# A fused attention and rational feed-forward kernel: first values in eight pieces by pairs of heads, products ordered by pairs, two small vectors from GpSimd's queue

## The chip, the cores and the metric

The kernel runs on one core of one Trainium2 chip. The metric is the device time of one execution in microseconds, as the median over several runs. Matrix products run on TensorE (PE in the profile, PEld for its weight loads), elementwise work on VectorE (DVE) and ScalarE (ACT), small set-up work on GpSimd (POOL). SyncE (SP) only issues loads and stores; ScalarE and GpSimd can issue them too, each from a queue of its own.

## The reference

The inputs are q, k and v of shape (4 batches, 4 heads, 1088 positions, 32), two sketch matrices S1 and S2 of shape (8, 32), two weight matrices w_in (128, 2048) and w_out (2048, 128), and two short vectors a (4 numbers) and b (2 numbers).

```python
def phi(x):
    a = np.einsum('rd,bhsd->bhsr', S1, x)
    b = np.einsum('rd,bhsd->bhsr', S2, x)
    return np.einsum('bhsi,bhsj->bhsij', a, b).reshape(*x.shape[:-1], r * r)
q_p, k_p = (phi(q), phi(k))
kv = np.einsum('bhsf,bhsd->bhfd', k_p, v)
z = np.sum(k_p, axis=2)
num = np.einsum('bhsf,bhfd->bhsd', q_p, kv)
den = np.einsum('bhsf,bhf->bhs', q_p, z)[..., None] + 1e-06
x = num / den            # then heads side by side: (4352, 128)
h = x @ w_in
P = a[0] + a[1] * h + a[2] * h**2 + a[3] * h**3
Q = 1.0 + np.abs(b[0]) * np.abs(h) + np.abs(b[1]) * h**2
out = (P / (Q + 1e-06)) @ w_out
```

The attention has no softmax: each batch first sums its keys and values into one small matrix (kv, with z as one more column), and then each query is multiplied by it.

## The kernel before

The kernel is written as named steps, and a long list, `ORDER` (L21 to L57), says in which order they are issued. A step `name:i` of the list calls one method for unit or block i. Every engine executes its own instructions strictly in the order of that list, and waits on semaphores for what another engine or a load has still to deliver. Nothing is reordered when the kernel runs.

**Keys** (class `Keys`). Batch 0 is treated in three parts of 2, 2 and 5 tile groups. `kt` transposes pieces of k on VectorE (L254); `ks` multiplies them by the sketch matrices on TensorE (L261); `kc` copies one half of the sketches on ScalarE (L268); `kf` multiplies both halves into the features k_p on VectorE (L273); `kp` multiplies features and values on TensorE and sums into kv (`products`, `add`, L302). `kk` copies kv to SBUF on ScalarE (tile kvz, L312). For batch 0 kv has two banks, one for each pair of heads (c = 0 and 1), and `kp0`, `kp1`, `kp2` each do one part for both pairs.

**Queries** (classes `Queries` and `Spread`). Blocks 0, 1, 2 of batch 0 have 256 positions each, block 3 has 320. `qt` transposes on VectorE (L325), `qs` sketches on TensorE (L338, for later blocks L409), `qc` copies on ScalarE (L345, L348, L415), `qf` makes the features on VectorE, `qp` multiplies by kvz (L365), `qd`, `qi`, `qx` divide (L373, L380, L385), `qb` transposes back on TensorE (L391), `qk` copies the result into xT on ScalarE (L398).

**Feed-forward.** Tokens come in units of at most 512. `h0` to `h3` compute quarters of the hidden layer on TensorE (L455, two wide PSUM buffers), `e0` to `e3` copy them to bf16 on ScalarE (L461); `u`, `w`, `y` form Q on VectorE; `ln`, `ex` form 1/Q on ScalarE; `pa`, `pd`, `s`, `m`, `v`, `x` form the terms of P/Q; `G` multiplies by w_out on TensorE (L588), `st` stores. The steps `wo:0` to `wo:5` (`w_part`) make the scaled bf16 copies of w_out, on ScalarE or VectorE by a table; `wo:0`, `wo:2`, `wo:4` use the first half of w_out, the others the second half. The step `ba` takes the absolute value of b (tile b_abs) on ScalarE.

**The opening.** Before the list, the loads of S1, S2, k, the first 512 columns of q, a, b and v are issued (L138 to L159). k comes in three loads over ScalarE's and SyncE's queues; then SyncE issues q and the four pieces of v (one for each quarter of the partitions, all four heads, `load_v`), and ScalarE issues a and b. GpSimd meanwhile fills masks and constants, and, when the sketch matrices are there, makes S21 (L206) and SAB (L212), the weights of the query sketches. The list then issues, on SyncE, the two halves of w_out (`lw:1`, `lw:0`), the rest of q (`lq:0`), the halves of w_in (`lx:1`, `lx:0`) and the loads of later batches (`lk`, `lv`, `lq`). The step `tn` (L167 to L170) runs matmuls on an empty tile, whose number is in `TURNS`, so that TensorE is not idle while the first loads are under way.

Completion of loads is counted on eight semaphores that the framework hands out in turn, over both hardware queues together. So a load is issued only when the load eight places before it has landed; on the queue of its engine, everything behind it waits too. Loads issued from GpSimd have counters of their own.

## Time and profile before

| what | value |
|---|---|
| median of 3 runs | 272.62 us (272.51 to 272.63) |
| profiled execution, whole | 272.61 us |
| its span, first to last instruction | 270.8 us |
| mean granted TensorE clock | 0.994 |
| busy time TensorE / VectorE / ScalarE / GpSimd | 257.7 / 256.7 / 248.8 / 2.9 us |
| busy in the first 10 us: TensorE / VectorE / ScalarE | 8.40 / 5.29 / 2.27 us |
| busy from 10 to 20 us: TensorE / VectorE / ScalarE | 9.95 / 7.65 / 5.02 us |
| moved by loads, 0 to 10 us and 10 to 20 us | 174 and 326 GB/s |

Busy time is a sum over all instructions of an engine. TensorE's includes the idle matmuls of the opening, and its matmuls overlap, so that a busy TensorE need not run at its peak. The profile's rows give start and length of an instruction (or of several of one line, merged), the line of the kernel, the operation, the tiles that it writes and reads, and in brackets how long the engine stood idle before it and what ended that. The chain of waits is read backwards: from the last instruction to what released it, and so on to the start; it is printed in order of time.

### The profile page before, as it was taken

What the parts mean: (1) busy time and instruction counts of PE and PEld (TensorE: products, weight loads), DVE (VectorE), ACT (ScalarE), POOL (GpSimd) and SP (SyncE); (2) the same over time, 40 slices, a digit from 0 to 9 for tenths busy, and PEclk for the clock granted to TensorE, in tenths of its full rate; (3) what the DMA queues carried; (4) which work ended last, traced back from release to release, by engine and by line L of the source; (5) the groups of instructions that cost most, each with busy time, mean ns of one, the idle gap of its engine ahead of it and who ended that gap; (6) DMA issues with size and microseconds to landing.
All of it is one profiled execution on the core that took longest, in us unless ns stands there. A gap on an engine that the chain in (4) does not pass through costs nothing.

```text
span 270.8 us, 3732 instructions
## 1 busy us (share of the span) xinstructions
PE 257.7 (95%) x1382; PEld 147.5 (54%) x1397; DVE 256.7 (95%) x278; ACT 248.8 (92%) x224; POOL 2.9 (1%) x24
## 2 busy tenths in 40 slices
PE   8999999999999899999999999999999999999683
PEld 3787556864645344635464554444545356675372
DVE  3777999999999999999999999999999999999994
ACT  1268999998999999999999999999999999999991
POOL 4000000000000000000000000000000000000000
PEclk9999999999999999999999999999999999999889
DMA  6995614333230044231304000400034200020005
GB/s 167 265 323 151 156 38 136 117 90 96 76 106 34 12 118 100 77 75 33 97 6 123 7 0 3 119 11 0 15 97 73 43 0 0 2 39 1 0 2 79
DMA packets 30530, 19.55 MB, mean 72 GB/s; under 512 B 20400, under 2 KB 26672, under 8 KB 30512
## 3 DMA queue, kind: packets, MB, share of 16 engines
q1 hardware_dynamic: 28864, 18.92, 26.9%
q10 hardware_dynamic: 1648, 0.40, 0.8%
q8 instruction: 11, 0.18, 0.3%
q14 instruction: 7, 0.06, 0.1%
HBM read 16.16 MB, written 3.15 MB: 71 GB/s over the span
## 4 chain that ended last, share of the span: by engine, by line
ACT 47%; PE 34%; issue 8%; DVE 5%; DMA 4%; SPq 0%; ACTq 0%; DVEq 0%
PE h_ps L455 16%; ACT ln L546 13%; ACT r L550 12%; ACT hh L461 12%; PE att_ps L588 10%; ACT p L541 7%; PE att_ps L365 3%; DMA v_sb<-in_v_dram 2%; PE att_ps L302 2%; DMA k_sb<-in_k_dram 2%; DVE g L558 2%; DVE s L554 1%; ACT xT L398 1%; PE att_ps L391 1%; PE att_ps L409 1%
## 5 line engine op out<-in xcount | busy, mean ns | idle before, releaser
L455 PE MATMUL h_ps<-xT,w_in_sb 128*128 128x512 f32 (+1 forms) x320 | 125.8, 537 | 2.8 <-ACT hh L461 1.9
L455 PEld LDWEIGHTS h_ps<-xT,w_in_sb 128*128 128x128 f32 x320 | 58.3, 190 | 55.2 <-issue 37.3
L461 ACT CAST hh<-h_ps 128x1024 bf16<-128x1024 f32 x68 | 67.5, 1027 | 3.5 <-PE h_ps L455 3.1
L588 PEld LDWEIGHTS <-w_out 128*128 128x128 bf16 x460 | 45.5, 100 | 45.9 <-issue 14.3
L546 ACT ACTIVATE ln<-w 128x2048 f32<-128x2048 bf16 (+1 forms) x35 | 66.0, 1887 | 0.7 <-DVE w L495 0.6
L550 ACT ACTIVATE r<-ln 128x2048 bf16<-128x2048 f32 (+1 forms) x35 | 65.8, 1880 | 0.6 <-PE att_ps L588 0.2
L541 ACT ACTIVATE p<-hh,a_sb 128x2048 bf16<-128x2048 bf16 (+1 forms) x23 | 46.7, 2035 | 0.1
L554 DVE TENSOR_TENSOR s<-hh,r 128x2048 bf16<-128x2048 bf16 (+2 forms) x33 | 41.0, 1246 | 0.2 <-ACT r L550 0.2
L495 DVE TENSOR_TENSOR w<-w,u 128x4096 bf16<-128x4096 bf16 (+2 forms) x22 | 39.4, 1798 | 0.1
L588 PE MATMUL att_ps<-g,w_out 128*128 128x512 bf16 (+1 forms) x154 | 34.8, 350 | 4.3 <-DVE g L569 3.9
L558 DVE TENSOR_TENSOR g<-hh,s 128x2048 bf16<-128x2048 bf16 (+1 forms) x30 | 35.2, 1175 | 0.0
L569 DVE TENSOR_TENSOR g<-g,p 128x2048 bf16<-128x2048 bf16 (+1 forms) x30 | 35.1, 1178 | 0.1
L588 PE MATMUL att_ps<-r,w_out 128*128 128x512 bf16 (+1 forms) x154 | 34.8, 353 | 0.3
L588 PE MATMUL att_ps<-s,w_out 128*128 128x512 bf16 (+1 forms) x137 | 29.3, 342 | 0.2
L490 DVE TENSOR_SCALAR w<-u,b_abs 128x4096 bf16<-128x4096 bf16 (+2 forms) x22 | 23.8, 1090 | 0.0
L484 DVE TENSOR_SCALAR u<-hh 128x4096 uint16<-128x4096 uint16 (+2 forms) x22 | 21.4, 976 | 1.6 <-ACT hh L461 1.5
L365 PEld LDWEIGHTS att_ps<-kvz,q_pT 128*128 128x128 f32 x144 | 17.7, 191 | 4.6 <-issue 2.0
L365 PE MATMUL att_ps<-kvz,q_pT 128*128 128x66 f32 x144 | 17.9, 273 | 0.1
L302 PEld LDWEIGHTS att_ps<-v_sb,k_p 128*64 128x64 f32 (+1 forms) x288 | 8.8, 138 | 1.9 <-DVE qT L325 0.8
L536 DVE TENSOR_SCALAR p<-hh,a_sb 128x2048 bf16<-128x2048 bf16 x12 | 9.7, 808 | 0.0
L302 PE MATMUL att_ps<-v_sb,k_p 128*64 128x64 f32 (+1 forms) x288 | 9.2, 223 | 0.5 <-DMA v_sb<-in_v_dram 0.5
L273 DVE TENSOR_TENSOR k_p<-att_ps,b_sk 128x1024 f32<-128x1024 f32 (+2 forms) x8 | 9.3, 1178 | 0.1
(60 smaller groups left out, 134.3 us busy)
## 6 DMA issues: line engine op xcount, KB each, us to landing
a_all<-sk_d SPq DMA_DIRECT2D x6, 384.0 KB
b_all<-sk_d SPq DMA_DIRECT2D x12, 192.0 KB
v_sb<-in_v_dram SPq DMA_DIRECT2D x12, 144.0 KB
k_sb<-in_k_dram SPq DMA_DIRECT2D x3, 544.0 KB
q_sb<-in_q_dram SPq DMA_DIRECT2D x3, 544.0 KB
a_all<-sk_d SPq DMA_DIRECT2D x4, 320.0 KB
b_all<-sk_d SPq DMA_DIRECT2D x8, 160.0 KB
w_out_sb_f<-in_moe_w_out_dram SPq DMA_DIRECT2D x2, 512.0 KB
```

What stands on the lines that cost most here:

```text
L365: nc.tensor.matmul(self.nd[:, o:o + 2 * KW], lhsT=self.q_p[:, c, x:x + 128], rhs=kvz[self.b % 2][:, c, :], start=True, stop=True)
L455: nc.tensor.matmul(t[:, x * tl:(x + 1) * tl], lhsT=w_in_sb[:, f * 128:(f + 1) * 128], rhs=xT[:, x_at(t0):x_at(t0) + tl], start=True, stop= ...
L461: nc.scalar.copy(out=live[i]["hh"][:, part * PW:(part + 1) * PW], in_=live[i]["h", part])
L490: nc.vector.tensor_scalar(out=t[:, c], in0=live[i]["u"][:, c], scalar1=ab1, scalar2=ab0, op0=AX.mult, op1=AX.add)
L495: nc.vector.tensor_mul(out=t[:, c], in0=t[:, c], in1=live[i]["u"][:, c])
L541: nc.scalar.activation(out=part_of(i, "p", h), in_=hh, func=ACT.Identity, scale=a3, bias=a2)
L546: nc.scalar.activation(out=t, in_=live[i]["w"][:, span(h)], func=ACT.Ln, bias=1.0 + 1e-6)
L550: nc.scalar.activation(out=part_of(i, "r", h), in_=live[i]["ln"], func=ACT.Exp, scale=-1.0)
L554: nc.vector.tensor_mul(out=part_of(i, "s", h), in0=hh, in1=part_of(i, "r", h))
L558: nc.vector.tensor_mul(out=part_of(i, "g", h), in0=hh, in1=part_of(i, "p" if horner(i, first(h)) else "s", h))
L569: nc.vector.tensor_mul(out=g, in0=g, in1=part_of(i, "s" if horner(i, first(h)) else "p", h))
L588: nc.tensor.matmul(outs[t0][:, :tl], lhsT=w_sb[y][:, f0 + x, :], rhs=part_of(i, key, h)[:, c:c + tl], start=done[0] == 0, stop=done[0] == ...
```

## The change

The first batch's values come in eight loads instead of four: each quarter of the partitions is split by pairs of heads. The four pieces of the first pair are issued before q, two from SyncE and two from ScalarE; the four pieces of the second pair are issued after q, all from SyncE. a and b are issued from GpSimd, behind the making of the identity matrix and ahead of S21 and SAB. `products` for batch 0 now does the first two parts for the first pair of heads (`kp0`), all three parts for the second pair (`kp2`), and the third part for the first pair (`kp1`); in the list `kp2` stands ahead of `kp1`.

In the list, `tn` has 9 + 2 = 11 idle matmuls instead of 11 + 2 = 13. `ks:0` stands ahead of `ks:1`, all key sketches and the features of the first two parts ahead of the first query's transpose and sketch, which now stands between `kp0` and `kp2`. The first half of w_out is loaded behind both halves of w_in; `wo:0`, `wo:2` and `wo:4`, which use it, stand later. `ba` stands ahead of the copy `qc:0`. Between there and the middle of the second unit some neighbours change places (the hidden quarters h1 and h0, the query blocks 5 and 6, `ln0:0` ahead of `kc1:1`); after that, single neighbours on different engines are exchanged, and three times two neighbours on ScalarE. The constant `VH` is not used.

```diff
-TURNS = (11, 0, 0, 0, 2, 0, 0, 0, 0)
+TURNS = (9, 0, 2, 0, 0, 0, 0, 0, 0)
 ORDER = """
-tn:4 tn:0 lw:1 lq:0 kt0:0 lw:0 kt1:0 lx:1 kt2:0 lx:0 ks1:0 kt3:0 ks0:0 lk:1 qt:0 ks2:0 kc0:0 kc1:0 kf0:0 kf1:0 qs:0
-kc2:0 qt:1 kf2:0 qc:0 kp0:0 ba:0 kp1:0 qf:0 kp2:0 wo:3 qs:1 kk:0 lv:1 qt:2 qp:0 qc:1 wo:1 qf:1 qs:2 qd:0 qi:0 qc:2
-qp:1 qx:0 qf:2 wo:0 qb:0 qp:2 qd:1 qi:1 qk:0 qx:1 qt:3 h3:0 qd:2 qi:2 lq:1 qx:2 wo:4 wo:2 h2:0 e3:0 kt1:1 h0:0 kt0:1
-e2:0 pa1:0 u1:0 lk:2 qs:3 w1:0 qb:2 h1:0 y1:0 qc:3 qk:2 e0:0 qt:5 qb:1 ks0:1 qt:4 e1:0 qs:4 qk:1 u0:0 ln1:0 h1:1 qt:6
...
+tn:0 lw:1 lq:0 tn:2 kt1:0 lx:1 kt0:0 lx:0 kt2:0 ks0:0 lw:0 ks1:0 kt3:0 kc0:0 lk:1 ks2:0 kf0:0 kc1:0 kf1:0 kp0:0 kc2:0
+qt:0 kf2:0 qs:0 ba:0 kp2:0 qt:1 qc:0 qf:0 kp1:0 wo:3 qs:1 kk:0 lv:1 qt:2 qp:0 qc:1 wo:1 qf:1 qs:2 qd:0 qi:0 qc:2 qp:1
+qx:0 qf:2 qb:0 qt:3 qp:2 qk:0 qd:1 lq:1 qi:1 h2:0 qd:2 qi:2 wo:2 wo:0 h3:0 wo:4 e2:0 qx:2 qx:1 kt1:1 qs:3 e3:0 kt0:1
+h1:0 pa1:0 u1:0 lk:2 w1:0 h0:0 y1:0 e1:0 qb:2 qt:4 qc:3 qb:1 e0:0 ks0:1 qt:6 qk:1 qs:4 u0:0 qk:2 ln1:0 h1:1 qt:5 w0:0
...
+    v0 = v[0].rearrange("h (g j) d -> g h (j d)", g=32)
+
+    def first_v(c):
+        for m in range(NM):
+            w = min(W, (NJ - m * NT) * D)
+            hs = slice(2 * c, 2 * c + 2)
+            (nc.scalar if c == 0 and m % 2 else nc.sync).dma_start(out=v_bufs[0][m * 32:(m + 1) * 32, hs, 0:w],
+                                                             in_=v0[:, hs, m * W:m * W + w])
+
     q0 = io.tile([128, S], FP, name="q_sb", bufs=1)
     q0_src = q[0].rearrange("h (g j) d -> (h g) (j d)", g=32)
+    first_v(0)
     nc.sync.dma_start(out=q0[:, 0:512], in_=q0_src[:, 0:512])
+    first_v(1)
     a_sb = consts.tile([128, 4], FP, name="a_sb")
     b_sb = consts.tile([128, 2], FP, name="b_sb")
-    nc.scalar.dma_start(out=a_sb, in_=bass.AP(tensor=moe_a.tensor, offset=moe_a.offset,
-                                              ap=[[0, 128]] + list(moe_a.ap)))
-    nc.scalar.dma_start(out=b_sb, in_=bass.AP(tensor=moe_b.tensor, offset=moe_b.offset,
-                                              ap=[[0, 128]] + list(moe_b.ap)))
     nc.scalar.preload_act_table_set("natural_log_exp_and_others")
-    load_v(0)
...
     make_identity(nc, ident)
+    nc.gpsimd.dma_start(out=a_sb, in_=bass.AP(tensor=moe_a.tensor, offset=moe_a.offset,
+                                              ap=[[0, 128]] + list(moe_a.ap)))
+    nc.gpsimd.dma_start(out=b_sb, in_=bass.AP(tensor=moe_b.tensor, offset=moe_b.offset,
+                                              ap=[[0, 128]] + list(moe_b.ap)))
...
             if self.first:
-                t0, n = self.PARTS[part]
-                self.add(part, range(t0, t0 + n), (0, 1))
+                for x in ((0, 1), (2,), (0, 1, 2))[part]:
+                    t0, n = self.PARTS[x]
+                    self.add(x, range(t0, t0 + n), (part // 2,))
```

## The prediction

> **What bounds the kernel now.** The profiled execution took 272.61 us, 270.8 us of it span and 1.8 us around it; the median of the three runs is 272.62 us, so a sum made against the profiled execution stands for the median too. I first read the page's table of slices and the busy time by stage:
>
> ```profile
> ACT  1268999998999999999999999999999999999991
> DMA  6995614333230044231304000400034200020005
> ```
>
> From the fourth slice on (slices are 6.8 us), ScalarE is nearly never free; between 30 and 50 us it is busy for 20.00 of 20 us, VectorE for 19.94. ScalarE's waits between 17 and 60 us are those for hidden layers at 19.60 and 21.33 and 0.2 us for a denominator. Saturated engines run the same work whenever they start, so what the opening gains or loses by about 21 us goes to the end one for one, unless something there comes at a fixed time. So next I read the chain of waits over the first 18 us (start, length, what):
>
> ```profile
> 1.48 4.35 DMA k_sb<-in_k_dram
> 5.83 0.02 issue
> 5.85 3.92 DMA v_sb<-in_v_dram
> 9.77 0.28 issue
> 10.05 2.32 PE att_ps L302 x72
> 12.37 1.06 PE h_ps L338 x8
> ...
> 17.66 0.40 PE h_ps L455
> ```
>
> k lands at 5.83, the last piece of v is issued in that moment and lands at 9.77; TensorE takes up the key products (L302) 0.28 us later and has no gap from there to the first hidden layer (L455). The timeline shows the work between:
>
> ```profile
> 5.00 0.15 PEld L170 LDWEIGHTS <-idle 128*128 128x128 bf16 x1 [0.28 <-issue]
> 5.07 1.62 DVE L254 STREAM_TRANSPOSE kT<-k_sb 128x256 f32<-128x256 f32 x4 [1.46 <-DMA k_sb<-in_k_dram]
> 5.43 0.15 PEld L170 LDWEIGHTS <-idle 128*128 128x128 bf16 x1 [0.27 <-issue]
> 6.41 1.00 PE L261 MATMUL att_ps<-S,kT 128*128 128x64 f32 x8
> 7.12 0.45 DVE L325 STREAM_TRANSPOSE qT<-q_sb 128x256 f32<-128x256 f32 x1 [0.43 <-DMA q_sb<-in_q_dram]
> 7.24 1.28 PE L261 MATMUL h_ps<-S,kT 128*128 128x64 f32 x10
> 7.69 1.29 DVE L273 TENSOR_TENSOR k_p<-att_ps,b_sk 128x512 f32<-128x512 f32 x2
> 8.45 1.13 PE L338 MATMUL h_ps<-qT,SAB 64*128 64x256 f32 x8
> 9.25 1.45 DVE L273 TENSOR_TENSOR k_p<-h_ps,b_sk 128x1280 f32<-128x1280 f32 x1
> 10.05 2.32 PE L302 MATMUL att_ps<-v_sb,k_p 128*64 128x64 f32 x72 [0.46 <-DMA v_sb<-in_v_dram]
> ```
>
> Two things can go: the 0.46 us for which TensorE waits for v, and its late start at 6.41, behind idle matmuls (L170), although the first two transposes (0.77 of the 1.62 us) are over at 5.84.
>
> **The change, step by step.** *Two idle matmuls fewer.* Their weight loads stand 0.43 us apart (5.00, 5.43), so idling ends up to 0.86 us sooner; the transposes let the sketches start at about 5.90: 0.51 us gained. The sketches take 6.41 to 8.45, 2.04 us, and end at 7.95.
>
> *Features before the query.* VectorE ends its transposes at 6.69. The first sketches now fill the first part alone, so its copy (L268, about 0.2 us) is done near 6.85, and both features are made by 6.9 + 1.29 = 8.2. Only then comes the query's transpose, to 8.2 + 0.37 (0.45 less its overlap) = 8.57. The wait for q of 0.43 us disappears if q lands by 8.2; it landed at 7.1 and has half of the first four v pieces, 144 KB, put ahead of it, 0.5 us at the 291 GB/s moved from 5.5 to 6.0 us. The large feature then ends at 8.57 + 1.45 = 10.02 instead of 10.70.
>
> *Products by pairs.* Half of the pieces now stand ahead of q, two on each queue, no longer behind k's landing. Their bytes lie right behind k's, so I put their landing near 7; TensorE wants them at 8.0. The eight products of two tile groups are done by about 8.5 (second feature 8.2). The query sketch starts at 8.63, takes its slot of 1.06 (chain, 12.37) and ends at 9.69. There remain 56 of 72 records; the stage fills 10.05 to 12.29, where the next begins, so 31 ns each: 1.74 us, to 11.43. The large feature sets no later end: 40 records after 10.02 is 11.3. Before, the end was 12.29: 0.86 us gained at most.
>
> *The last piece of v.* Each load is issued when the load eight places before it has landed, as the fourth piece was, at 5.85. The last two now follow the first v piece and the rest of k. I put that piece at 6.2 to 6.4 (k's 5.83 and half a piece: the second load of v moved its four in the 2.4 us from 52.8 to 55.2, 0.3 us each half), so the last issue starts at about 6.8. From an issue's start to use I have two rows: about 2.0 us in the second load (last issue at 53.2, data moving until 55.2) and 3.92 in the chain. That gives 8.8 to 10.7; I take 9.55, nearer the lower, as pieces are half as large and less stands ahead. With the chain's 0.28 us, products restart at 9.83, end at 11.57: a gain of 0.72 us. The ends of the range are 0.86 (landing by 9.4) and 12.29 - (10.98 + 1.74) = -0.43.
>
> A rule against it stands in the Trainium skill, "DMA: Bandwidth & Descriptors", section Bandwidth: under 64 KB a transfer costs mostly its fixed part, 64 KB taking 0.95 us and 1 MB 6.15. By it, as an estimate, eight pieces of 72 KB take 8.0 us and four of 144 KB 5.6, 2.4 more if nothing overlaps. In the second load four such pieces moved in 2.4 us all told, so pieces overlap and the trace does not agree.
>
> *a and b from GpSimd.* Their two issue slots on ScalarE's queue (0.45 and 0.44) go to two pieces of v: nothing saved there. On GpSimd they stand before S21 and SAB (L206, L212). No row shows a load issued there; by the nearest, a slot costs from 0.44 to 1.33 us (the longest issue, w_in's first). GpSimd is idle for 1.03 us before L206, so SAB, ready at 4.76, comes by 6.4 at worst; the query sketch at 8.63 covers it, and past that each us late is one us lost. Landing: b is now read ahead of the query copy, at about 9.75, a at 11.48. Issued by 5.3 at the latest, b lands between 7.3 (the 2.0 of above) and 12.3 (7.0 us, the time from its issue at 3.09 to its use at 10.12, in which it never made anyone wait). I take the lower, as any other load of the opening took under 4 us where nothing lay ahead; cost 0. At the upper end the query copy and the kvz copies behind it on ScalarE start at 12.5, kvz ends at 13.65, and the products that waited until 13.36 lose 0.3.
>
> *w_out's first half behind w_in.* The queue's data: 174 GB/s over the first 10 us, then 326. k, q, v, both halves of w_out and w_in and the rest of q are 3.72 MB, all moved by 16.1; the first half of w_out, by the same sum at 10.5, was used at 11.48, so the lag is 1.0 and the second arrives at about 17.1, at most 18. Behind it wait ScalarE's scaling (1.16 us), moved from 16.09 to after the first xT copy, into the idle stretch 17.88 to 19.60, and on VectorE two more (1.43 us) ahead of the quotients of the second and third query blocks (0.42 each). These end by 18 + 2.3 = 20.3 and are needed by the transposes at 23.37. Cost 0; with the cover gone, from about 18.5, each us costs up to one.
>
> *Next in line.* Everything from 12.29 moves up by 0.72. The second part of q, landed for the transpose at 12.36 to 12.81, serves a sketch at 14.39 that moves to 13.67: 0.86 us left. Batch 1's keys come at 20.12, behind which VectorE waited 0.88 us for ScalarE anyhow. The remaining neighbours exchanged later are the same instructions in the same load: 0.
>
> Sum: 272.61 - 0.72 = **271.9 us**.
>
> **Rivals.** *The last piece lands no sooner.* For it: v waits for bytes ahead, and the DMA share is near 1 from 3.0 to 7.5 us. Against: it is 0.54 at 8.0 to 9.0. Then products restart at 10.05, end at 11.79: gain 0.50, 272.1. Chance 0.10.
>
> *Given back in the next stage:* w_out's half at 19 holds ScalarE until 20.2, the hidden copy that was ready at 20.6 is pushed to 21.2 by the one before it, and of 0.72 remain 0.1: 272.5. For it: the queue is full from 10 to 20 us (share 1.06). Against: the sum above gives 18 at most. Chance 0.10.
>
> *Slower: each smaller piece costs what a larger one did.* Eight at 0.6 us are 2.4 more of moving; free DMA time between 7.5 and 9.5 (shares 0.77, 0.54, 0.54, 0.56) takes 0.8 of it, so the last lands up to 9.77 + 1.6 = 11.4. It turns to a loss from 10.27 (12.29 - 1.74 - 0.28); in the middle, 10.8, products end at 12.82: 273.1.  Chance 0.12.
>
> *Slower: TensorE stays at its first pace.* Idle matmuls go at 0.43 us; only the last two took 0.33 and 0.22 (weight loads at 5.86 and 6.19, sketches at 6.41). Eleven instead of thirteen end at 5.9, just as the sketches come; a gap there could leave TensorE at the first pace as long again, 4.7 us. Its 3.6 us of sketches and products would double: about 275. Against: TensorE has worked from 1.19 without a gap. Chance 0.06. The Trainium skill, "TensorE: Matmul & The Clock Gate", Part 1, says the same of a free-running window of 3.4 us that must be busy; by it, as an estimate, a missed window loses its half, 1.7 us, and nothing is lost if the sketches follow at once.
>
> **How the numbers follow.** The forecast has 0.62, with an own range of 271.65 to 272.15. A difference under 0.2% (0.55 us) cannot be told from none by a measurement of this kernel. Faster by more: 0.54 of the forecast's 0.62. Within: its other 0.08 and the first two rivals, 0.28. Slower: 0.18. The range runs from 271.4, where both gains come whole (0.97) with 0.2 to spare for the unknown, to 273.1, the middle of the slow rival.
>
> **What would show it.** Right: sketches at about 5.9; no gap over 0.2 us before L302's first records near 8.1; the query sketch between the pairs; the last products done near 11.5; the first L455 near 16.85; and the start of saturation on ScalarE earlier by about 0.7. Wrong: VectorE waiting for q at 8.2, TensorE waiting for v past 10, ScalarE or VectorE held by a, b or w_out, matmuls at 0.43 us after 6.1, or a gain at 21 us that is gone at 60.

## The result, and the profile after

The changed kernel takes 273.40 us (median of 11 runs, 272.80 to 274.48); the kernel before, on the same chip, 272.65 (11 runs, 272.51 to 273.12). The ratio is 1.0025, with a 95% interval of 1.0015 to 1.0036. In a second measurement it was 273.26 (12 runs) against 272.57, ratio 1.0024 (1.0013 to 1.0035). So the change costs 0.7 us; the forecast was a gain of 0.7.

The profiled execution took 273.80 us with a span of 272.0, 0.40 above the median. The timeline of its first 13 us (start, length, engine, line, what; in brackets the idle time before it and what ended that) answers to the one shown of before:

```profile
5.50 0.77 DVE L265 STREAM_TRANSPOSE kT<-k_sb 128x256 f32<-128x256 f32 x2 [1.87 <-DMA k_sb<-in_k_dram]
6.32 1.10 PE L272 MATMUL att_ps<-S,kT 128*128 128x64 f32 x8 [0.26 <-DVE kT L265]
6.64 0.84 DVE L265 STREAM_TRANSPOSE kT<-k_sb 128x480 f32<-128x480 f32 x2 [0.38 <-DMA k_sb<-in_k_dram]
8.79 0.69 PE L314 MATMUL att_ps<-v_sb,k_p 128*64 128x64 f32 x16
8.99 0.45 DVE L337 STREAM_TRANSPOSE qT<-q_sb 128x256 f32<-128x256 f32 x1 [0.34 <-DMA q_sb<-in_q_dram]
9.36 1.45 DVE L284 TENSOR_TENSOR k_p<-h_ps,b_sk 128x1280 f32<-128x1280 f32 x1
10.65 1.85 PE L314 MATMUL att_ps<-v_sb,k_p 128*64 128x64 f32 x56
...
12.43 0.49 PE L350 MATMUL h_ps<-qT,SAB 64*128 64x256 f32 x2
```

The order of the work is the new one: 16 products of the first pair, then the query, then the other 56. But k came late here (its transposes start at 5.50 instead of 5.07), and the next sketch (L350) starts at 12.43, 0.14 later than before. Further on, the chain of waits up to 25 us (start, length, what) has left TensorE:

```profile
2.35 5.15 DMA v_sb<-in_v_dram
7.50 0.02 issue
7.51 0.31 SPq L156
...
10.39 9.36 DMA w_out_sb_f<-in_moe_w_out_dram
19.75 0.02 issue
19.77 1.15 ACT w_out L635
20.92 1.82 ACT hh L473 x2
22.75 0.02 issue
22.77 2.10 ACT p L553
```

It runs from the first piece of v, for which SyncE waits before it can issue on, through six issues to w_out's first half, and that load takes 9.36 us from its issue to its landing at 19.75. ScalarE's timeline at that place:

```profile
16.96 0.37 ACT L410 COPY xT<-att_ps 128x256 f32<-128x256 f32 x1 [0.62 <-PE att_ps L403]
17.83 0.18 ACT L388 ACTIVATE den<-att_ps 128x8 f32<-128x8 f32 x1 [0.50 <-PE att_ps L377]
19.77 1.15 ACT L635 ACTIVATE w_out<-w_out_sb_f,a_sb 128x1024 bf16<-128x1024 f32 x1 [1.77 <-DMA w_out_sb_f<-in_moe_w_out_dram]
20.83 1.91 ACT L473 CAST hh<-h_ps 128x1024 bf16<-128x1024 f32 x2
22.77 2.10 ACT L553 ACTIVATE p<-hh,a_sb 128x2048 bf16<-128x2048 bf16 x1
```

ScalarE stands for 1.77 us until w_out's half is there, and the two hidden copies queue behind the scaling. Before, the first polynomial (p) started at 22.37; now at 22.77. Compared instruction by instruction, ScalarE lags by 0.40 us here and by 0.72 to 0.73 from about 37 us to the end. VectorE also waits 0.96 us for batch 1's keys at 22.75; that this wait makes up the rest of the lag is likely, and no run tests it. The last 0.5 us of the difference in span is behind the last computation. The last output transpose and the issues of the last stores (least, median and greatest length in ns, first and last start in us), first of the kernel before:

```profile
267.13 0.45 DVE L597 STREAM_TRANSPOSE out_sb<-att_ps 128x256 f32<-128x256 f32 x1 [0.69 <-PE att_ps L588]
L605 SPq DMA_DIRECT2D out_dram<-out_sb x10: 316/450/507, 263.3 to 268.0; - x10
L605 ACTq DMA_DIRECT2D out_dram<-out_sb x2: 380/422/463, 267.6 to 268.0; - x2
```

and of the changed kernel:

```profile
267.85 0.45 DVE L609 STREAM_TRANSPOSE out_sb<-att_ps 128x256 f32<-128x256 f32 x1 [0.69 <-PE att_ps L600]
L617 SPq DMA_DIRECT2D out_dram<-out_sb x10: 315/448/512, 264.0 to 269.0; - x10
L617 ACTq DMA_DIRECT2D out_dram<-out_sb x2: 378/420/463, 268.3 to 268.8; - x2
```

The transpose is 0.72 later, SyncE's last store 1.0. From the end of that transpose to the end of the span it was 3.24 us and is 3.71. I call this stretch the end.

So three things were suspected: w_out's half behind w_in; the loads from GpSimd's queue, as k was late; and the four more pieces on SyncE's queue, behind which all large loads were issued 1.2 us later (8.34 instead of 7.11).

### The profile page after: what moved, and what is told of

Read it like the earlier page. It is cut to its first block, busy times and chain, and to the rows that moved or that the text cites. A ratio compares the mean times of both kernels' runs of the same rounds, so it can differ in the third digit from the quotient of the medians.

```text
span 272.0 us, 3752 instructions
## 1 busy us (share of the span) xinstructions
PE 257.6 (95%) x1395; PEld 146.5 (54%) x1395; DVE 256.1 (94%) x278; ACT 249.1 (92%) x224; POOL 4.1 (2%) x26
## 4 chain that ended last, share of the span: by engine, by line
ACT 41%; PE 34%; issue 8%; DMA 7%; DVE 6%; SPq 3%; DVEq 0%; ACTq 0%
PE h_ps L467 16%; PE att_ps L600 12%; ACT hh L473 12%; ACT ln L558 11%; ACT r L562 10%; ACT p L553 6%; DMA w_out_sb_f<-in_moe_w_out_dram 3%; DMA v_sb<-in_v_dram 3%; PE att_ps L377 2%; DVE g L570 2%; DVE s L566 1%; DVE w L507 1%; SPq L617 1%; PE att_ps L421 1%; PE att_ps L314 1%
## 5 line engine op out<-in xcount | busy, mean ns | idle before, releaser
L600 PEld LDWEIGHTS <-w_out 128*128 128x128 bf16 x460 | 44.9, 99 | 46.6 <-issue 14.9
L600 PE MATMUL att_ps<-s,w_out 128*128 128x512 bf16 (+1 forms) x140 | 30.0, 342 | 0.1
```

The lines of the kernel that those rows point to most:

```text
L600: nc.tensor.matmul(outs[t0][:, :tl], lhsT=w_sb[y][:, f0 + x, :], rhs=part_of(i, key, h)[:, c:c + tl], start=done[0] == 0, stop=done[0] == ...
```

## The experiments

All times are medians, with the ratio to the kernel before, measured on the same chip, and its 95% interval.

### First four: which part of the change

**a and b not loaded** (`a_no_ab_load`):

```diff
-    nc.gpsimd.dma_start(out=a_sb, ...)
-    nc.gpsimd.dma_start(out=b_sb, ...)
+    nc.gpsimd.memset(a_sb, 0.3)
+    nc.gpsimd.memset(b_sb, 0.3)
```

> The changed kernel with a and b filled with 0.3 on GpSimd instead of loaded (their values are wrong, all else is the same). Theory G (GpSimd's two loads slow the queue while k is under way, 92 GB/s from 3 to 4 us instead of 188): k lands as before, the first transposes start at 5.1 instead of 5.50, the later ones at 5.85 instead of 6.64, v and the bulk loads follow 0.4 to 0.8 us sooner, the time falls by at least 0.4 us to 273.0 or less. Theory Q (the second pair's pieces hold SyncE's queue until 8.3, each waiting for a load eight places ahead): transposes again at 5.5, time 273.4. Theory W (w_out's first half behind w_in is what costs): 273.4.

273.03 us, ratio 1.0022 (1.0009 to 1.0035). In its profile the products end sooner than in the changed kernel (the next stage's sketch starts at 11.98), but w_out's half landed at 19.94, ScalarE waited 2.41 us for it and p started at 22.96. Whatever the opening gained was gone there.

**Two more loads of a and b, from GpSimd, in the kernel before** (`b_ab_also_gpsimd`), into tiles that nothing reads:

```diff
     make_identity(nc, ident)
+    nc.gpsimd.dma_start(out=a_too, ...)
+    nc.gpsimd.dma_start(out=b_too, ...)
```

> The kernel before with two more loads of a and b from GpSimd, into tiles that nothing reads. Theory G: k lands 0.4 to 0.8 us late, first transposes at about 5.5, time 0.3 to 0.8 us above before. Theories Q and W: k at 5.05 as before, no difference in time.

273.43 us, 1.0036 (1.0021 to 1.0051): these loads alone cost as much as the whole change. The opening ran 0.27 later (first hidden layer at 17.84 instead of 17.57), batch 1's keys came at 22.24. At this point GpSimd's loads looked guilty.

**w_out's first half ahead of w_in again** (`a_w_out_first`):

```diff
-... kt1:0 lx:1 kt0:0 lx:0 kt2:0 ks0:0 lw:0 ks1:0 ...
+... kt1:0 lw:0 kt0:0 lx:1 kt2:0 ks0:0 lx:0 ks1:0 ...
```

> The changed kernel with the first half of w_out loaded ahead of w_in, as before. Theory W: ScalarE's scaling no longer waits until 19.77, its hidden copies start 1 us sooner and the time falls by 0.4 us or more, to 273.0 or less. Theories G and Q: ScalarE gains its 0.4 us at 22 us, but VectorE still gets batch 1's keys at 22.7 instead of 20.1 and is as late as in the changed kernel, so the time stays at 273.3 to 273.4.

272.86 us, 1.0013 (1.0004 to 1.0022): 0.54 less than the changed kernel's first median of 273.40 and 0.40 less than its second, 273.26, though the intervals of the ratios touch (the changed kernel's began at 1.0013 in the second measurement). ScalarE's timeline:

```profile
17.32 1.14 ACT L635 ACTIVATE w_out<-w_out_sb_f,a_sb 128x1024 bf16<-128x1024 f32 x1
19.10 1.01 ACT L473 CAST hh<-h_ps 128x1024 bf16<-128x1024 f32 x1 [0.64 <-PE h_ps L467]
20.82 1.01 ACT L473 CAST hh<-h_ps 128x1024 bf16<-128x1024 f32 x1 [0.71 <-PE h_ps L467]
21.87 2.09 ACT L553 ACTIVATE p<-hh,a_sb 128x2048 bf16<-128x2048 bf16 x1
```

The scaling lies in the idle stretch that the prediction had meant for it, and p starts 0.50 us ahead of the kernel before. The last transpose is 0.41 ahead (266.72). But the end takes 3.72 us instead of 3.24, so the profiled execution comes out at 272.67, no better than before.

**One load per head over all partitions** (`a_four_loads`), four in all:

```diff
+        for h in (2 * c, 2 * c + 1):
+            (nc.scalar if h == 1 else nc.sync).dma_start(
+                out=v_bufs[0][:, h, 0:W],
+                in_=bass.AP(tensor=v.tensor, offset=v.offset + h * S * D, ap=[[W, NM], [S * D // 32, 32], [1, W]]))
```

> The changed kernel with one load per head over all 128 partitions (heads 0 and 1 ahead of q from SyncE and ScalarE, heads 2 and 3 behind q), four loads instead of eight, 64 columns more per row in the last quarter that no product reads. Theory Q: no load of SyncE waits past 6 us, w_out's second half is issued by about 6.2 instead of 8.34, all bulk loads land 1 us or more sooner, batch 1's keys by 20.5, time 272.2 or less. Theory G: k is still late (transposes at 5.5 and 6.6), time 273.0 or more.

277.54 us, 1.0181 (1.0168 to 1.0195): the expectation of a gain was far off. SyncE is free from 5.1 us and issues the large loads at once, and v is late:

```profile
4.13 10.05 DMA v_sb<-in_v_dram
...
14.23 2.47 PE att_ps L313 x54
```

The last load of v is down at 14.18, 10.05 us after its issue. The form of the loads is the likely cause: the trace shows each of them landing in four parts, where the loads of k, q and the weights land in sixteen, as many as there are DMA engines. (The outer dimension of these loads of v is four.) So the first batch's v seems to have passed through four engines, while the others had less to do: the mean busy share of the sixteen was 0.63 from 6 to 7 us and 0.57 from 10 to 11. The large loads had four late parts as well: of w_out's second half, issued at 5.14, twelve parts were down at 9.70 to 10.40 and four at 15.32 to 15.54. TensorE stood for 2.78 us in this opening, and its granted clock was then 0.50 from 13 to 15 us. This run does not try theory Q, because it changes the form of v's loads as well as their number: whether SyncE's waiting behind four loads of the usual form is a loss stays open.

### Second four: one part alone

**w_out's first half last, in the kernel before** (`b_w_out_last`):

```diff
-... lq:0 kt0:0 lw:0 kt1:0 lx:1 kt2:0 lx:0 ...
+... lq:0 kt0:0 lx:1 kt1:0 lx:0 kt2:0 lw:0 ...
```

> The kernel before with one part of the change alone: w_out's first half is issued behind both halves of w_in instead of ahead of them; all else as before. Theory W (the new place in the queue is a cost by itself, wherever the other loads stand): the half lands near 18.2 us instead of 13.95, ScalarE stands at its scaling from 16.1 to 18.2, and what it then lacks reaches the saturated stretch: 273.0 to 273.2. Theory L (the place costs only because all large loads are 1.2 us later in the changed kernel; at 18.2 the idle stretch of ScalarE from 17.88 to 19.60 covers it): 272.65, within 0.2.

276.72 us, 1.0133 (1.0098 to 1.0168), far more than either theory had. The half was used at 18.54. In the order of the kernel before, the copy of xT stands behind the scaling, so TensorE stood idle, and then it was slow. TensorE's row, and lengths (least/median/greatest, ns) of the hidden layer's matmuls from 19.9 to 23 and from 23 to 26 us:

```profile
20.00 7.01 PE L455 MATMUL h_ps<-xT,w_in_sb 128*128 128x256 f32 x24 [2.31 <-ACT xT L398]
```

```profile
L455 PE MATMUL h_ps<-xT,w_in_sb x7: 617/631/792, 20.0 to 22.7; 128*128 128x256 f32 x7
```

```profile
L455 PE MATMUL h_ps<-xT,w_in_sb x15: 379/379/617, 22.7 to 26.0; 128*128 128x256 f32 x15
```

After 2.31 us of idling the matmuls take 631 ns instead of 379 for 2.7 us: 24 of them fill 7.01 us instead of 5.45. The granted clock was 0.50 from 20 to 23 us and 0.90 in the next. The 4.0 us by which p is late are 2.4 of waiting and 1.6 of this. The changed kernel, with its scaling behind xT, avoids it.

**a and b moved to GpSimd, in the kernel before** (`b_ab_moved`):

```diff
-    nc.scalar.dma_start(out=a_sb, ...)
-    nc.scalar.dma_start(out=b_sb, ...)
...
     make_identity(nc, ident)
+    nc.gpsimd.dma_start(out=a_sb, ...)
+    nc.gpsimd.dma_start(out=b_sb, ...)
```

> The kernel before with one part of the change alone: a and b are loaded by GpSimd's queue and no longer by ScalarE's. Theory G (two small loads on GpSimd's queue slow the loads of the other queues from 2.6 us on, and what is late there reaches batch 1's keys): 273.1 to 273.5, with keys of batch 1 past 21.5 (20.12 before), as with the two added loads (273.43). Theory N (not that a load is on GpSimd's queue but two loads more is what cost there): 272.65, keys at 20.1.

273.26 us, 1.0026 (1.0017 to 1.0035), as theory G had it. The profile splits it differently: the opening is 0.26 later and stays so to the last transpose (267.38 instead of 267.13), and the end takes 3.67 instead of 3.24. The edit does one thing more, however: with two loads fewer on the eight counters, SyncE issues v's last two pieces at 3.82 and 4.29 instead of 5.07 and 5.85, and w_out's second half at 5.16 instead of 7.11. So GpSimd's queue and the earlier issues are not told apart here.

**Whole pieces** (`a_whole_pieces`): w_out's half ahead, and v in four pieces of four heads, all ahead of q.

```diff
-            hs = slice(2 * c, 2 * c + 2)
+            hs = slice(0, 4)
...
-    first_v(1)
```

> The changed kernel with w_out's first half ahead of w_in again, and the first values in four pieces of four heads each (144 KB), all ahead of the first part of q, two on each queue; the order of products and all else as changed. Theory P (four more pieces hold SyncE's queue, so the large loads are issued 1.2 us later, and batch 1's keys come late): the large loads are issued from about 7.1 again, batch 1's keys land by 20.5, 272.2 to 272.5. Theory G (GpSimd's loads make the keys of batch 1 late, however many pieces there are): keys past 21 again and 272.8 to 273.0. If the large loads take the queue from v, as with four loads over 128 partitions: v after 10.5, over 273.2.

275.92 us, 1.0118 (1.0084 to 1.0152). Neither theory had this. VectorE's row shows who is late:

```profile
10.29 0.45 DVE L336 STREAM_TRANSPOSE qT<-q_sb 128x256 f32<-128x256 f32 x1 [1.67 <-DMA q_sb<-in_q_dram]
```

With 72 KB pieces q landed at 8 to 9; behind 144 KB pieces, and beside a large load issued at 5.24, it lands at 10.26, and the features of the last part stand behind its transpose. So what was won by splitting v is lost when its pieces are large and a large load goes beside them; which of the two delays q this run does not tell apart.

**a and b later on GpSimd** (`a_ab_late`), with w_out's half ahead:

```diff
-    nc.gpsimd.dma_start(out=a_sb, ...)
-    nc.gpsimd.dma_start(out=b_sb, ...)
...
         SAB.append(t.rearrange("p a i j -> p (a i j)"))
+    nc.gpsimd.dma_start(out=b_sb, ...)
+    nc.gpsimd.dma_start(out=a_sb, ...)
```

> The changed kernel with w_out's first half ahead of w_in again, and a and b issued on GpSimd's queue only behind S21 and SAB (near 5 us instead of 2.6), b first. Theory G: the loads of k are as fast as without a and b (parts at 5.1 and 6.0), products end 0.3 us sooner and the time is 272.4 to 272.6, unless b itself lands past 10 and holds the query copy, which would give 272.9. Theory P: GpSimd's loads do not set the end; 272.86 within 0.15, keys of batch 1 still near 21.2.

273.44 us, 1.0030 (1.0018 to 1.0042): no gain. k's parts landed at 5.23 and 6.34, no sooner than with the loads early. Its last transpose is 0.22 ahead of before, and its end takes 4.04. From here on the end was a suspect of its own.

### Third four: the end

Counted in the trace, the instruction of SyncE that has 207 others ahead of it started 0.33 to 0.65 us late in the executions at hand where that could be seen. In the kernel before it is a wait at the end for a store that has not landed by then; in the changed kernel, which issues more on SyncE, it is the last store.

**Two more small loads on SyncE, in the kernel before** (`b_two_small`):

```diff
     def fetch_v(b):
+        for n in range(2 if b == 3 else 0):
+            nc.sync.dma_start(out=consts.tile([128, 4], FP, name=f"a_too{n}"), in_=...)
```

> The kernel before with two more 2 KB loads on SyncE's queue at the load of batch 3's values, into tiles that nothing reads. In all profiles so far SyncE's instruction that has 207 others ahead of it starts some 0.35 us late: in the kernel before it is a wait at the end that is hidden behind the landing of the stores, in the changed kernel it is the last store. Theory T (the place of the last store in SyncE's list of instructions decides): two more instructions make the last store that one here too, the two last stores of SyncE stand 0.69 us apart instead of 0.36, the stores land 0.3 us later, and the time is 272.9 to 273.1. Theory P (the late last store has to do with the eight pieces or with GpSimd's loads): 0.36 us apart, 272.65 within 0.15.

273.17 us, 1.0020 (1.0012 to 1.0029). The time is as theory T had it, the sign is not: the list grew by three, the last two stores of SyncE stand 0.37 us apart. The end takes 3.63 us all the same, and this execution's opening is 0.28 late with no load on GpSimd's queue at all.

**One more small load in the changed kernel** (`a_one_small`), the same edit with `1 if b == 3`.

> The changed kernel with one more 2 KB load on SyncE's queue at the load of batch 3's values, into a tile that nothing reads. Theory T: the late instruction is now the last store but one of SyncE, which waits for the last transpose anyhow; the last two stores stand 0.36 us apart, and the time falls by 0.3 to about 273.05 although there is one load more. Theory P: 0.69 apart as before, 273.4 or a little more.

272.91 us, 1.0013 (1.0000 to 1.0026), below the changed kernel with one load more, though its interval overlaps with that one's. The stores stand 0.38 apart, but in the profiled execution (273.33) the end still takes 3.90 us.

**One store from ScalarE** (`a_w_out_first_end`), with w_out's half ahead:

```diff
-(nc.scalar if t0 + tl == n_tok and e % 2 else nc.sync)
+(nc.scalar if (t0 + tl == n_tok and e % 2) or (i == 14 and e == 3) else nc.sync)
```

> The changed kernel with w_out's first half ahead of w_in again, and one of the last stores but four (the fourth quarter of unit 14) issued by ScalarE instead of SyncE, so that SyncE has one instruction fewer ahead of its last store. Theory T: the opening's gain of 0.41 us that the last instructions of the version without the store's move showed is no longer eaten by the late store: end of the last transpose to end of span 3.3 us instead of 3.7, and the time is 272.3 to 272.5, below both kernels. Theory P: 272.86 again.

272.82 us, 1.0014 (0.9993 to 1.0036). Stores 0.36 apart, the end 3.55 us; the profiled execution is at 272.46 as theory T had it, the median is not.

**The same without loads of a and b** (`a_w_out_first_end_no_ab`).

> As the run before it, and a and b are not loaded but set to 0.3 on GpSimd, so that the output is another. It shows what the two loads on GpSimd's queue cost once w_out and the end are mended. Theory G (they slow k by 0.1 to 0.4 us, and two more counters are waited for and cleared at the end, 0.11 us together): 0.2 to 0.5 us under the run before it, 271.9 to 272.2. Theory K (batch 1's keys, not the opening, set the time now): at most the 0.11 of the end.

272.91 us, 1.0004 (0.9993 to 1.0014). The profiled execution, 271.92, was the lowest of its 12 runs: k at 4.67 and 5.60, the last transpose 0.91 ahead of before. The median shows no gain over the run before. So without the loads of a and b k can be early, but it was as early with them in the second profile of the changed kernel, shown next, and late without them in `a_no_ab_load` (5.18 and 6.35): theory G does not explain the opening.

### The next four: kernel or execution

**The changed kernel again** (`after_again`) **and the kernel before again** (`before_again`).

> The changed kernel itself once more, for a second profile. Theory L (its loss is made by late loads in the first 23 us and at the last store): w_out's first half past 19 us again, batch 1's keys past 22, the last two stores of SyncE 0.69 us apart, 273.2 to 273.6. Should k's parts land at 5.0 and 6.1 as with w_out's half moved back, and not at 5.5 and 6.6, then that part of the first profile was chance.

> The kernel before once more, for a second profile: keys of batch 1 at 20.1 within 0.5, end of the last transpose to end of span 3.2 us within 0.1, if these two readings are of the kernel and not of the one execution.

273.26 us for the changed kernel (profiled: 273.56) and 272.61 for the one run of the kernel before. In this second profile the opening gains what was forecast, and a little more:

```profile
4.73 0.77 DVE L265 STREAM_TRANSPOSE kT<-k_sb 128x256 f32<-128x256 f32 x2 [1.07 <-DMA k_sb<-in_k_dram]
5.56 1.10 PE L272 MATMUL att_ps<-S,kT 128*128 128x64 f32 x8
7.87 0.69 PE L314 MATMUL att_ps<-v_sb,k_p 128*64 128x64 f32 x16
9.66 1.85 PE L314 MATMUL att_ps<-v_sb,k_p 128*64 128x64 f32 x56
11.44 1.14 PE L350 MATMUL h_ps<-qT,SAB 64*128 64x256 f32 x8
```

The next stage starts at 11.44 instead of 12.29: 0.85 us gained. ScalarE, a little later:

```profile
19.30 1.15 ACT L635 ACTIVATE w_out<-w_out_sb_f,a_sb 128x1024 bf16<-128x1024 f32 x1 [2.29 <-DMA w_out_sb_f<-in_moe_w_out_dram]
20.36 1.91 ACT L473 CAST hh<-h_ps 128x1024 bf16<-128x1024 f32 x2
22.30 2.10 ACT L553 ACTIVATE p<-hh,a_sb 128x2048 bf16<-128x2048 bf16 x1
```

Of 0.85, 0.07 is left: p at 22.30 instead of 22.37. w_out's half landed at 19.28. And the end takes 4.06 us, with the last two stores of SyncE 0.69 apart; the keys came at 21.76, a little sooner than expected. As for the kernel before, its second profile has the same end (3.29) and the same p (22.40), although batch 1's keys came at 21.46 instead of 20.10, which the expectation had not allowed for: VectorE can wait that long without loss.

**Batch 1's keys ahead of w_in's second half** (`a_keys_early`), with w_out's half ahead and the store moved:

```diff
-... lx:0 ks1:0 kt3:0 kc0:0 lk:1 ...
+... ks1:0 kt3:0 kc0:0 lk:1 lx:0 ...
```

> The changed kernel with w_out's first half ahead of w_in, one store moved to ScalarE as in a run before, and the keys of batch 1 issued ahead of the second half of w_in instead of behind it. Theory K (with w_out mended, VectorE's wait of 1.9 us for these keys sets the time): keys by 20, w_in's second half by 21.4, just at its use; no wait of VectorE over 0.5, 272.2 to 272.5. Theory E (the keys do not set it; what the opening gains is lost in run to run differences of the landings): 272.8 again.

272.82 us, 1.0010 (0.9999 to 1.0021), the same as without. The keys came at 18.61 and VectorE no longer waited for them; w_in's second half came at 21.68, and TensorE waited 0.44 us for it at 21.81. Theory K falls: the wait moved from one load to the other.

**a and b from ScalarE again** (`a_all_mended`), else as the run before:

```diff
     nc.scalar.preload_act_table_set("natural_log_exp_and_others")
+    nc.scalar.dma_start(out=a_sb, ...)
+    nc.scalar.dma_start(out=b_sb, ...)
+    first_v(1)
...
-    nc.gpsimd.dma_start(out=a_sb, ...)
-    nc.gpsimd.dma_start(out=b_sb, ...)
```

> As the run before it, and a and b on ScalarE's queue again, behind its table load and ahead of the second pair's pieces, so that nothing is loaded by GpSimd's queue. Theory G: k at 4.7 and 5.6, opening 0.5 us sooner, no sixth wait at the end, 271.8 to 272.2, below the kernel before. Should ScalarE's wait for k's landing at its load of b hold the first copies, then 0.3 more. Theory E: 272.5 to 272.8.

273.79 us, 1.0042 (1.0026 to 1.0058). k landed at 5.07 and 6.16, as with GpSimd's loads; the two issues pushed the second pair's pieces back (second one issued at 6.99), and every large load with them: the first half of w_in landed at 17.93 and the hidden layer, which waited 0.54 us, started at 18.04. No version came out below the kernel before.

### Last two: why w_out's half is so late

A load lands in sixteen parts. From the landings in the trace, for w_out's first half (us):

```
                            first   15th    16th    TensorE's code load starts
kernel before               13.23   13.92   13.95   15.00
changed kernel              17.12   18.46   19.75   15.07
changed kernel again        16.01   17.30   19.28   14.35
a_no_ab_load                16.81   18.24   19.94   15.24
b_w_out_last                16.01   16.75   18.52   14.45
```

TensorE's code is loaded by DMA as well. The queues of the second profile of the changed kernel from 14 to 21 us (packets, MB, share of 16 engines):

```profile
q1 hardware_dynamic: 1841, 2.09, 108.5%
q8 instruction: 1, 0.02, 0.9%
```

The one packet of q8 is 16 KB of code, 0.97 us long, in the midst of a queue that is full. Fifteen parts of w_out's half were down at 17.30 in the second profile of the changed kernel, inside the forecast of 17.1 to 18; one was not. Seventeen executions can be compared so (the parts of `a_four_loads` are apart for the reason told above). In them, 46 large loads had landed before TensorE's first load of code of 16 KB (the queue q8 in the profile) began: their last part came at most 0.46 us after the fifteenth, 0.17 in the median. For the 56 that landed behind its start it was up to 2.9 us, and 0.80 in the median.

**The code load moved** (`a_early_code`, and `b_early_code` for the kernel before, with 84 + 6 small idle matmuls instead of 11 + 2 large ones):

```diff
-TURNS = (9, 0, 2, 0, 0, 0, 0, 0, 0)
+TURNS = (78, 0, 6, 0, 0, 0, 0, 0, 0)
...
-            nc.tensor.matmul(idle_ps[:, :cols], lhsT=idle[:, 0:128], rhs=idle[:, :cols], start=True, stop=True)
+            nc.tensor.matmul(idle_ps[0:32, :cols], lhsT=idle[:, 0:32], rhs=idle[:, :cols], start=True, stop=True)
```

with `cols` 32 instead of 512.

> The changed kernel with 84 small idle matmuls (32 x 32) in place of 11 large ones, for TensorE to have about 146 more instructions ahead of the first sketch. In every profile a 16 KB load of TensorE's instructions starts when it has issued some 255 to 285 of them, at 13 to 16 us, in the midst of the large loads; of a load's sixteen parts the last then lands up to 2.9 us behind the fifteenth, where loads that were down by then have at most 0.46 (w_out's first half in the second profile of the changed kernel: fifteen parts by 17.30, the last at 19.28). Theory F (that code load holds one of the sixteen DMA engines): it moves to about 9.5 to 10.5 us, the fifteen parts of w_out's first half land about as before, the last within 0.6 us of them, ScalarE's wait for it shrinks from 1.8 to 2.3 us to under 1, and the time falls by 0.3 to 0.8, if the small matmuls keep TensorE's pace; at its first pace the sketches and products lose up to 1.5. Theory O (one DMA engine is late for another reason, such as the share that v's second load gives it): the gap stays 1.3 to 2.

> The kernel before with 90 small idle matmuls in place of 13 large ones, for the price of the small ones by themselves and for the same code load. Theory F: the last parts of w_in's second half and of batch 1's keys land within 0.6 us of the fifteenth (0.63 and 0.46 in the first profile, 1.85 and 1.86 in the second), and since nothing waited for them long, the time stays at 272.65 within 0.3 unless TensorE is at its first pace for longer. Theory O: gaps as before.

The code load moved to 7.66 and 6.07 us, sooner than expected. The last part of w_out's first half came 0.15 us after the fifteenth (18.77 and 18.92), that of batch 1's keys 0.11; the delay went to the pieces of v that were under way instead: 1.23 us on three of the second pair in the one kernel, 1.05 on the first piece in the other. So a load of code delays one part of the loads of its moment, as theory F says. Three things keep it from being the whole answer. The code takes about 1 us, and w_out's last part is late by up to 2; in the changed kernel's first profile the code was over at 16.12, and the distance of the last part still grew from 0.67 us (the load down at 17.38) to 1.29 (19.75) and 1.89 (22.73). In `a_w_out_first` and `a_ab_late`, whose code came at 13.57 and 13.84, the halves of w_out and w_in that landed behind its start had at most 0.61 and 0.44. And in these two runs the second batch's v was issued later too (from 16.1 and 14.8 us, instead of 11.5 to 12.5 in the two kernels), so theory O is not quite excluded. The times, 275.86 (1.0118, 1.0100 to 1.0135) and 275.76 (1.0110, 1.0093 to 1.0127), have another cause: the small matmuls were over at 3.6 us, and TensorE, idle for 2.30 us, went on at a slow pace, 1.97 us for eight sketches that took 1.00 in the kernel before and 1.10 in the changed one:

```profile
5.91 1.97 PE L272 MATMUL att_ps<-S,kT 128*128 128x64 f32 x8 [2.30 <-DVE kT L265]
```

## Why the prediction was wrong

It was made of an opening and of an argument that what the opening gains is kept. The opening's steps came as described, but what they gained hung on when k landed; the argument failed at one step, and a second loss was not in the sum at all.

*Two idle matmuls fewer; features before the query; products by pairs.* Right where k lands early: sketches at 5.56 in the second profile (forecast 5.90), first products at 7.87 (8.1), the query sketch between the pairs at 8.59 (8.63). The wait for q did not quite vanish: q, with four pieces of v ahead of it on two queues where the sum counts 144 KB, landed at 7.98, VectorE waited 0.21. In the first profile k landed 0.8 to 0.9 us later than in the second, and everything with it. k's first part landed between 4.67 and 5.47 in the executions of kernels with these eight pieces of v, and no part of the change explains which; the forecast took k as fixed. So the forecast gain was met by luck: in the five versions with k's first part at 5.00 to 5.09, as before, the next stage's sketch started at 11.69 to 12.04, a gain of 0.25 to 0.60 us. A part of what is missing there is the change's own: k's second part followed its first by 0.94 to 1.17 us in the eleven executions with the eight pieces, and by 0.78 to 0.85 in the seven with the loads of the kernel before.

*The last piece of v.* Put at 9.55; it landed at 8.84 and 9.93. The remaining 56 products started at 9.66 and 10.65, right behind the query sketch, which had waited for q and its transpose (8.00 and 8.99), and not for v. The stage ended 0.85 sooner and 0.14 later, where 0.72 was forecast. The rival of small pieces costing as much as large ones is out: all eight were down by 9.93 at the latest.

*a and b from GpSimd.* They landed at 7.24 and 7.87, or 8.36 and 9.16, and nobody waited for them. So 0 was right as far as the opening shows. They do add a sixth wait to SyncE's chain at the end (0.065 us) and lengthen the last clearing of semaphores by 0.05.

*w_out's first half behind w_in: the failed step.* "Arrives 17.1, at most 18 ... Cost 0." It arrived at 19.28 and 19.75, and the price was the one that the step itself named for that case, nearly one for one: 0.78 of 0.85 us in the second profile. Two things were mis-sized. The arrival was worked out from the bytes of the whole queue, as if a load were there when the mean of the sixteen engines has moved it; but its last part decides, and that one came 1.3 to 2.0 us after the fifteenth. A load of code ran while this load was under way, and such a load delays one part, as shown above; how that comes to as much as 2 us stays open. (The fifteen parts alone would have been late too in the first profile: 18.46, with 18 as the latest forecast.) In the kernel before the half had landed at 13.95, a good microsecond ahead of the code load at 15.00, and could not show a late part; but the two loads behind it in that very profile could have: w_in's second half with 0.63 between its last two parts, the keys with 0.46. Two slips in the working are small beside this: by the sizes of its loads the sum of 3.72 MB is 3.77, about 0.15 us more, and the half used at 11.48 is the one that the list calls second, which landed at 11.46. And the slack was counted to 18.5 from a row of the kernel before, while an opening that is sooner by 0.85 needs the half sooner by as much.

The Trainium skill, "DMA: Bandwidth & Descriptors", section "Why a DMA increments its semaphore by 16 and not by 1", says that an intermediate count does not tell which bytes have come, and that only the full sixteen mean that the data is down. The traces agree: the scaling started 0.02 us after the sixteenth part, 2.00 after the fifteenth.

*The rival "given back in the next stage"* had the mechanism and the place: the half at 19, ScalarE held until 20.2, 0.1 of 0.72 left, 272.5. In the second profile it was 19.28, 20.45 and 0.07. What lies between 272.5 and 273.3 is for the most part the end.

*The end* was in no term. The prediction said that whatever is gained by 21 us goes to the end one for one, and up to the last transpose that held only roughly: 0.07 ahead at p and 0.11 behind at the transpose in the second profile, 0.40 and 0.72 behind in the first (0.14 of it from the opening, 0.26 lost up to p, 0.33 on the way to the transpose), 0.50 and 0.41 ahead in the version with w_out's half moved back. Behind it the changed kernel loses 0.47 and 0.82 us. In six executions, in all of which SyncE's last store is the instruction with 207 others ahead of it, it was issued 0.69 us after the one before, in the others 0.35 to 0.38 us; that is 0.33 of the loss. GpSimd's two counters are 0.11. The rest are single late parts of the last stores, and their cause was not found.

*Why moving w_out's half back is still no gain.* In that version's profile the opening is 0.44 us sooner (the next stage's sketch at 11.85), p 0.50 and the last transpose 0.41, so nothing is given back; the end takes 0.48 of it. With the store moved the end is 0.17 shorter, but the medians of the two versions are the same within their intervals. And w_in has lost its slack: its first half lands 0.14 us ahead of its first use (16.96 and 17.10), where before it had 1.64 (15.93 and 17.57). From 10 to 20 us the queue is full in both kernels; in `a_keys_early`, where the keys were put ahead, it was w_in's second half that came late.

The other rivals: TensorE at its first pace did not occur in the changed kernel (idle for 0.26 us at most in the opening), but the runs with small idle matmuls show its price, 275.8 where 275 was forecast. The last piece landing no sooner did not happen either.

## What to carry to other kernels

When the work of an opening is pulled forward, the loads behind it do not come sooner: put each large load's landing beside its new time of need, and take the landing from the sixteenth part and not from bytes by a mean rate. A step that is free before is free because of slack, and the slack shrinks by what the change gains ahead of it. A tuned kernel can also lose at its other end: compare the time from the last computation to the end of the span in both profiles before looking for causes in the changed part.

## What the runs showed of the hardware that was not expected

- A load of TensorE's code delays one of the sixteen parts of the loads that are under way. It has 16 KB, is about 1 us long and starts, in eighteen of the twenty executions, when some 240 to 285 of TensorE's instructions are done (13 to 17 us here), and in the two with small idle matmuls after 185 to 189. When 146 more instructions put it at 7.66 us, loads of that moment had their last part 1.23 us late, and w_out's half and the keys behind it 0.15 and 0.11. Large loads behind the code had their last part late by anything from 0.01 to 2.9 us, and what sets the size was not found.
- TensorE slows after a short idle stretch: after 2.31 us (`b_w_out_last`) its matmuls took 631 ns instead of 379 for 2.7 us. The Trainium skill, "TensorE: Matmul & The Clock Gate", Part 1, puts the fall of the clock after at least one idle window of about 3.4 us; here 2.31 us were enough, and the measured number decides.
- The end of a program is part of its time, and it changes with what SyncE and GpSimd have issued: the four executions with the kernel before's own steps on SyncE and nothing loaded by GpSimd (`before`, `before_again`, `b_w_out_last`, `b_early_code`) took 3.23 to 3.29 us from the last transpose to the end, the sixteen others 3.42 to 4.06. In all twenty the SyncE instruction with 207 others ahead of it started at least 0.37 us after the end of the one before it. Two 2 KB loads that nobody needs, in the middle of the kernel before, cost 0.20% (0.12 to 0.29).
- A load's form can set in how many parts it lands. v's loads with an outer dimension of four (`a_four_loads`) landed in four parts instead of sixteen; the last of them took 10.05 us, and of w_out's second half, issued behind the others, four parts came 5 us after the other twelve.
